# The product of the minus rows read from PSUM, a one-hot written once, powers of two for four rows at once

## The chip, the cores and the metric

The kernel runs on one core of a Trainium2 chip. Its time is the device time of one execution in microseconds (us), the median of 3 runs. Five engines work side by side and wait for each other through semaphores: PE (TensorE, matrix products; PEld is its loading of weights), DVE (VectorE), ACT (ScalarE), POOL (GpSimd) and SP (SyncE, which here only issues DMAs). PE writes its results to PSUM, eight banks of 128 x 512 float32; the other data of a core lies in SBUF.

## What is computed

```python
x  = real(fft(fft(x, axis=seq), axis=dim))       # x: 8 x 3072 x 256, float32
a, b = x @ w_a, x @ w_b                          # 256 -> 1536 each
y  = (a * b) @ w_out                             # 1536 -> 256, for 24576 rows
e  = argmax(y @ w_gate)                          # one of 8 experts for each row
out[row] = gate * sigmoid(..) * (relu(y @ w1[e]) @ w2[e])
```

## The kernel before

The first part makes, for each of 8 batches, the transform, then a and b, their product, and y with its gate; the second part (from about 2140 us) runs the experts over the rows sorted by expert. The change lies in the first part.

A real input makes the transform's rows come in pairs, position n and position S - n. From two matrix products one gets both: with U and V the two halves of a row of a, `E + O` is the row of the plus side and `E - O` the one of the minus side. So a tile is 512 positions and yields 1024 rows, 24 tiles in all, and each is worked through in 12 steps of 128 columns of a and b (f = 0 to 11), 288 steps. A step uses one of two pairs of PSUM banks, `s[0]` for a and `s[1]` for b; steps take the pairs in turn. On the engines a step (function `step`) is:

- PE: 3 products of 128x512 into the bank of a and 3 into that of b (`products(..., 0)`, L831): now the banks hold the first halves. Then `g2` (L904): 24 products of 128x256, which give y for an earlier step. Then again 3 and 3 products onto the same banks (`products(..., 1)`): now the banks hold the rows of the plus side.
- DVE, between these, for the step before (`first`) and for this one: AM[0] and AM[1] (L840), the minus rows of a and of b, each 2E less the plus row, from EE in SBUF and the bank in PSUM; hf[0] (L841), the product of the plus rows, from the bank of a and BP, a copy of the bank of b that ACT makes (L837); EE[0], EE[1] (L871), the even parts of this step's a and b, read from its banks, after which PE may write onto these banks again; hf[1] (L846, in `first_minus`), the product of the minus rows, from AM[0] and AM[1], both in SBUF.
- ACT rounds hf to float16 (L851), POOL takes the remainder hf - hl (L853, 128x1024), and `g2` of a later step uses both.

Work that belongs to other tiles or batches is dealt out beside the steps: `deal` puts an item into the first unit (a step, or one of the transform's units, called D) where its estimated costs on ACT, DVE, POOL and SP fit a budget. Such items are: the splitting of the next batch (L512 to L599), of the experts' weights (L406 to L470), and for each finished tile the rows' squares (L940), powers of two near them (`pow2`, L159 and L160), rows (L951, L957), gates (L992 to L1034) and places (L1051 to L1061). Each engine runs its instructions in the order written: within a unit the DVE's items come after hf[1].

Some of PE's items in the middle of `g2` (the logits L972, the counts L1038, the spreads L820, L388, L437) write into a bank called `aux`: the bank of a of the step before, whose last reader is hf[0].

Of the kernel before, what the change touches and what calls it, by code (L numbers as in the profile page):

```python
# [12 lines left out]
ACTF = mybir.ActivationFunctionType  # L13
ALU = mybir.AluOpType
# [27 lines left out]
def chain_kernel(ctx, tc, x, x384, w_a, w_b, w_out, w_gate, w_og, w1, w2, dft, c16, c32, ids, out):  # L42
# [11 lines left out]
    # One stretch of SBUF for the whole run: the second part keeps the experts in it,  # L54
    # the first part lays its own operands over the same places.
# [167 lines left out]
    def rows384():  # L223
        # the row that folds onto itself, of every batch: sums of its four places with their signs
# [26 lines left out]
    def from64(ts, jobs):  # L251
        # float64 to float32 by its bits; below float32's normal range it becomes 0
# [376 lines left out]
    # positions 4k, then the odd ones, then 4k + 2  # L629
# [115 lines left out]
    # the rows of position S / 2, one of each batch: all their products at once  # L745
# [63 lines left out]
    def tile_src(T):  # L809
        t, j0, nj = T  # L810
        if t == NTILE:
            return UVm, 1
        c0 = 512 * (t % 3) + 128 * j0
        return UV[:, (t // 3) % 2, :, c0:c0 + 128 * nj], 2
# [13 lines left out]
    def products(s, src, n, fs, uv):  # L828
        for ab in range(2):
            for i, (a, h) in enumerate(((0, 0), (0, 2), (1, 0))):  # L830
                pe.matmul(out=s[ab][:, 0:n], lhsT=Wt[:, ab, uv, a, fs], rhs=src[:, h + uv, :], start=(uv == 0 and i == 0), stop=(i == 2), skip_group_check=(uv == 1))  # L831

    def first(P):
        s, n, ns = P["s"], P["n"], P["ns"]
        P["hf"] = three.tile([128, 2, 512], FP32, tag="hf", name="hf")
        P["B"] = BP
        act.activation(out=P["B"][:, 0:n], in_=s[1][:, 0:n], func=ACTF.Copy)  # L837
        if ns == 2:
            for ab in range(2):
                dve.scalar_tensor_tensor(out=AM[:, ab, 0:n], in0=P["E"][:, ab, 0:n], scalar=2.0, in1=s[ab][:, 0:n], op0=ALU.mult, op1=ALU.subtract)  # L840
        dve.scalar_tensor_tensor(out=P["hf"][:, 0, 0:n], in0=s[0][:, 0:n], scalar=CA * CA, in1=P["B"][:, 0:n], op0=ALU.mult, op1=ALU.mult)  # L841

    def first_minus(P):
        n = P["n"]
        if P["ns"] == 2:
            dve.scalar_tensor_tensor(out=P["hf"][:, 1, 0:n], in0=AM[:, 0, 0:n], scalar=CA * CA, in1=AM[:, 1, 0:n], op0=ALU.mult, op1=ALU.mult)  # L846

    def second(P):
        n, ns, hf = P["n"], P["ns"], P["hf"]
        hl = hlp.tile([128, 2, 2, 512], FP16, tag="hl", name="hl")  # L850
        act.activation(out=hl[:, 0, 0:ns, 0:n], in_=hf[:, 0:ns, 0:n], func=ACTF.Copy)  # L851
        run("pool0")
        (dve if n == 128 else pool).tensor_tensor(out=hl[:, 1, 0:ns, 0:n], in0=hf[:, 0:ns, 0:n], in1=hl[:, 0, 0:ns, 0:n], op=ALU.subtract)  # L853
        hq.append((P["T"], P["f"], hl, ns))

    def step(T, f, job):
        src, ns = tile_src(T)
        n = 128 * T[2]
# [4 lines left out]
        P = {"s": s, "n": n, "ns": ns, "T": T, "f": f}  # L863
        products(s, src, n, fs, 0)
        if prev:
            first(prev[0])
        if ns == 2:
            P["E"] = EE
            c0 = 128 * T[1]
            for ab in range(2):  # L870
                dve.scalar_tensor_tensor(out=P["E"][:, ab, 0:n], in0=st_x[T[0]][:, c0:c0 + n], scalar=w0[:, ab, f:f + 1], in1=s[ab][:, 0:n], op0=ALU.mult, op1=ALU.add)  # L871
# [17 lines left out]
        products(s, src, n, fs, 1)  # L889
# [8 lines left out]
    def g2(T, f, hl, ns):  # L898
        nj = T[2]
        nt = nj * ns  # L900
# [10 lines left out]
    def post_items(T):  # L911
# [91 lines left out]
        def gate2():  # L1003
# [4 lines left out]
            oh = new("oh", 8)  # L1008
# [9 lines left out]
            if nt < 8:  # L1018
                dve.memset(oht[:, 0:8, :], 0.0)
            dve.tensor_copy(out=oht[:, 0:nt, :], in_=oh)  # L1020
# [26 lines left out]
        def place():  # L1047
# [9 lines left out]
            if first_ or t == NTILE:  # L1057
                bd = baddm if t == NTILE else badd0
                dve.tensor_tensor(out=df[:, 0:nt], in0=df[:, 0:nt], in1=bd[:, 0:nt], op=ALU.add)
            st["di"] = two.tile([128, 8], I32, tag="di", name="di")  # L1060
            dve.tensor_copy(out=st["di"][:, 0:nt], in_=df[:, 0:nt])  # L1061
# [12 lines left out]
        for a in range(0, nt, 2):  # L1074
            n_ = min(nt, a + 2) - a
            items.append((0 if a else 1, [("act", 0.43 * n_, c(square, a, a + 2)), ("dve", 0.3, c(power, a, a + 2))]))
# [192 lines left out]
    with tc.manual_schedule():  # L1269
# [4 lines left out]
        # start: the first batch and the weights  # L1274
# [160 lines left out]
        # dealing of the work beside the products  # L1435
# [63 lines left out]
        # the units  # L1499
# [366 lines left out]
```

## Time and profile before

| | |
|---|---|
| time, median of 3 (lowest to highest) | 3094.85 us (3092.26 to 3096.49) |
| span of the profiled execution | 3101.2 us |
| busy over the span: PE / DVE / ACT / POOL | 93% / 74% / 42% / 44% |
| first part: steps with L831, L871, L846 | 100 to 2025 us of the span |

The profiled execution is one more execution of the same program, with no time of its own beside the span, which runs from its first instruction to its last; so the span stands for it. It is 6.35 us over the median of the three timed runs. L12 is line 12 of the kernel; `out<-in` names the tiles that an instruction writes and reads.

### The profile page before, as it was taken

What the parts mean: (1) busy time and instruction counts of PE and PEld (TensorE: products, weight loads), DVE (VectorE), ACT (ScalarE), POOL (GpSimd) and SP (SyncE); (2) the same over time, 40 slices, a digit from 0 to 9 for tenths busy, and PEclk for the clock granted to TensorE, in tenths of its full rate; (3) what the DMA queues carried; (4) which work ended last, traced back from release to release, by engine and by line L of the source; (5) the groups of instructions that cost most, each with busy time, mean ns of one, the idle gap of its engine ahead of it and who ended that gap; (6) DMA issues with size and microseconds to landing.
All of it is one profiled execution on the core that took longest, in us unless ns stands there. A gap on an engine that the chain in (4) does not pass through costs nothing.

```text
span 3101.2 us, 62225 instructions
## 1 busy us (share of the span) xinstructions
PE 2884.3 (93%) x24101; PEld 2179.5 (70%) x24101; DVE 2293.7 (74%) x4210; ACT 1307.2 (42%) x2605; POOL 1371.9 (44%) x1083
## 2 busy tenths in 40 slices
PE   6899899989899979989989999989999999999998
PEld 3566655756566656556666666678888888888898
DVE  8779699788999778999967999935555555555556
ACT  4444455535445445445454444432333333333332
POOL 6466577465774546674524445422211111111122
PEclk8899999999999999999999999999999999999999
DMA  5321712541221362221162222445222222222211
GB/s 196 109 59 42 179 56 66 138 109 44 76 71 44 103 140 59 57 89 42 52 164 80 64 61 69 103 128 149 57 52 52 52 51 51 53 52 53 50 45 35
DMA packets 363575, 244.46 MB, mean 79 GB/s; under 512 B 303101, under 2 KB 320669, under 8 KB 362382
## 3 DMA queue, kind: packets, MB, share of 16 engines
q1 hardware_dynamic: 342158, 184.75, 24.0%
q0 software_dynamic: 18816, 51.54, 4.8%
q10 hardware_dynamic: 2304, 4.20, 0.5%
q8 instruction: 188, 3.08, 0.4%
q14 instruction: 109, 0.89, 0.1%
HBM read 106.60 MB, written 70.33 MB: 57 GB/s over the span
## 4 chain that ended last, share of the span: by engine, by line
PE 56%; DVE 23%; issue 10%; DMA 4%; ACT 3%; POOL 2%; SPq 0%; DVEq 0%; POOLq 0%; ACTq 0%
PE g L1613 16%; PE g L1637 15%; PE s L831 10%; PE y L904 10%; DVE EE L871 6%; DVE hf L846 4%; PE s L662 2%; DVE AM L840 2%; DVE ohx L1020 1%; DVE rows L957 1%; DMA big<-in_dft_dram 1%; POOL hl L853 1%; DVE hf L841 1%; ACT BP L837 1%; DMA rows<-rows,di 1%
## 5 line engine op out<-in xcount | busy, mean ns | idle before, releaser
L831 PE MATMUL s<-big 128*128 128x512 f16 x3456 | 817.3, 387 | 99.2 <-DVE EE L871 89.9
L853 POOL TENSOR_TENSOR hl<-hf,hl 128x1024 f16<-128x1024 f32 x288 | 628.5, 2182 | 576.5 <-ACT hl L851 528.8
L904 PE MATMUL y<-big,hl 128*128 128x256 f16 x6912 | 822.4, 274 | 1.2 <-POOL hl L853 1.1
L904 PEld LDWEIGHTS <-hl 128*128 128x128 f16 x6912 | 672.2, 98 | 152.6 <-issue 10.8
L831 PEld LDWEIGHTS <-big 128*128 128x128 f16 x3456 | 341.3, 99 | 476.7 <-issue 141.9
L851 ACT ACTIVATE hl<-hf 128x1024 f16<-128x1024 f32 x288 | 303.9, 1055 | 560.4 <-DVE hf L846 463.9
L1640 POOL DMA_INDIRECT out_dram<-o,di x189 | 194.3, 1028 | 777.9 <-ACT o L1639 524.6
L1613 PE MATMUL g<-yt,w1t 128*128 128x256 f16 (+1 forms) x4704 | 492.8, 265 | 3.7 <-DVE w1t L1594 3.7
L1637 PE MATMUL g<-w2t,hh 128*128 128x256 f16 x2896 | 479.5, 273 | 0.0
L1613 PEld LDWEIGHTS <-w1t 128*128 128x128 f16 x4704 | 431.5, 98 | 50.8 <-DVE w1t L1594 4.0
L840 DVE SCALAR_TENSOR_TENSOR AM<-EE,s 128x512 f32<-128x512 f32 x576 | 382.3, 681 | 111.0 <-ACT BP L837 79.3
L1616 DVE SCALAR_TENSOR_TENSOR hl<-g,hh 128x512 f16<-128x512 f32 x378 | 260.2, 691 | 239.3 <-ACT hh L1615 239.3
L1637 PE MATMUL g<-w2t,hl 128*128 128x256 f16 x1448 | 394.9, 273 | 0.0
L1615 ACT ACTIVATE hh<-g 128x512 f16<-128x512 f32 x378 | 225.0, 597 | 275.9 <-PE g L1613 275.9
L1065 POOL DMA_INDIRECT rows<-rows,di x192 | 204.1, 1063 | 266.7 <-DMA rows<-rows,di 206.7
L1637 PEld LDWEIGHTS <-hh 128*128 128x128 f16 x3024 | 294.5, 98 | 34.2
L1598 DVE COPY w2t<-big 128x4104 f16 x98 | 120.5, 1229 | 205.4 <-PE g L1637 205.4
L846 DVE SCALAR_TENSOR_TENSOR hf<-AM 128x512 f32<-128x512 f32 x288 | 266.7, 926 | 0.0
L1639 ACT ACTIVATE o<-g,sc 128x256 f32<-128x256 f32 x189 | 89.5, 473 | 410.7 <-PE g L1637 357.8
L871 DVE SCALAR_TENSOR_TENSOR EE<-big,w,s 128x512 f32<-128x512 f32 x288 | 200.8, 738 | 0.0
L871 DVE SCALAR_TENSOR_TENSOR EE<-xe,w,s 128x512 f32<-128x512 f32 x288 | 200.7, 737 | 0.0
L841 DVE SCALAR_TENSOR_TENSOR hf<-s,BP 128x512 f32<-128x512 f32 x288 | 196.2, 681 | 0.0
(330 smaller groups left out, 2859.4 us busy)
## 6 DMA issues: line engine op xcount, KB each, us to landing
big<-in_x_dram SPq DMA_DIRECT2D x48, 514.0 KB
big<-in_dft_dram SPq DMA_DIRECT2D x60, 384.0 KB
big<-in_moe_w_dram SPq DMA_DIRECT2D x16, 1024.0 KB
wsc<-big SPq DMA_DIRECT2D x32, 512.0 KB
big<-wsc SPq DMA_DIRECT2D x7, 2050.0 KB
big<-in_dft_dram SPq DMA_DIRECT2D x60, 192.0 KB
big<-wsc ACTq DMA_DIRECT2D x16, 256.2 KB
raw<-in_moe_w_out_dram SPq DMA_DIRECT2D x6, 512.0 KB
```

Of the source, the lines that this page charges most:

```text
L831: pe.matmul(out=s[ab][:, 0:n], lhsT=Wt[:, ab, uv, a, fs], rhs=src[:, h + uv, :], start=(uv == 0 and i == 0), stop=(i == 2), skip_group_che ...
L840: dve.scalar_tensor_tensor(out=AM[:, ab, 0:n], in0=P["E"][:, ab, 0:n], scalar=2.0, in1=s[ab][:, 0:n], op0=ALU.mult, op1=ALU.subtract)
L841: dve.scalar_tensor_tensor(out=P["hf"][:, 0, 0:n], in0=s[0][:, 0:n], scalar=CA * CA, in1=P["B"][:, 0:n], op0=ALU.mult, op1=ALU.mult)
L846: dve.scalar_tensor_tensor(out=P["hf"][:, 1, 0:n], in0=AM[:, 0, 0:n], scalar=CA * CA, in1=AM[:, 1, 0:n], op0=ALU.mult, op1=ALU.mult)
L851: act.activation(out=hl[:, 0, 0:ns, 0:n], in_=hf[:, 0:ns, 0:n], func=ACTF.Copy)
L853: (dve if n == 128 else pool).tensor_tensor(out=hl[:, 1, 0:ns, 0:n], in0=hf[:, 0:ns, 0:n], in1=hl[:, 0, 0:ns, 0:n], op=ALU.subtract)
L871: dve.scalar_tensor_tensor(out=P["E"][:, ab, 0:n], in0=st_x[T[0]][:, c0:c0 + n], scalar=w0[:, ab, f:f + 1], in1=s[ab][:, 0:n], op0=ALU.mul ...
L904: pe.matmul(out=Y[w // 2][:, w % 2, :], lhsT=hl[:, h, pm, 128 * j:128 * j + 128], rhs=wo[:, f, a, :], start=(f == 0 and i == 0 and w % 2 = ...
L1613: pe.matmul(out=ps[:, u, :], lhsT=w[:, a, q, 128 * f:128 * f + 128], rhs=yt[:, 2 * h + q, :], start=(m == 0), stop=(m == 5))
L1615: act.activation(out=hh[:, f0:f0 + nu, :], in_=ps, func=ACTF.Relu)
L1616: dve.scalar_tensor_tensor(out=hl[:, f0:f0 + nu, :], in0=ps, scalar=0.0, in1=hh[:, f0:f0 + nu, :], op0=ALU.max, op1=ALU.subtract)
L1637: pe.matmul(out=ps, lhsT=hx[:, f, ts], rhs=wv[:, a, f, :], start=(m == 0), stop=(m == 3 * NF2 - 1))
```

## The change

The minus row of b is no longer written to AM[1] in SBUF but in place into the bank of b in PSUM, and the product of the minus rows reads it there, with AM[0] as its other operand. AM[0] still goes to SBUF. The order becomes AM[0], hf[0], the minus row of b, EE[0], EE[1], hf[1]. The one-hot of the experts is written in float16 at once, into the tile that the counting product reads, and the later readers take it from there; the copy with a change of type (L1020) goes. The places are written as integers by the addition itself, or by a maximum of the float value with itself where nothing is added; the copy L1061 goes. The powers of two are made for four rows in a pair of instructions rather than for two. Cases for tiles other than 512 positions, which the plan doesn't make, are taken out of the step's functions.

```diff
@@ -807,11 +807,8 @@
         return cur["aux"][0]
 
     def tile_src(T):
-        t, j0, nj = T
-        if t == NTILE:
-            return UVm, 1
-        c0 = 512 * (t % 3) + 128 * j0
-        return UV[:, (t // 3) % 2, :, c0:c0 + 128 * nj], 2
+        t = T[0]
+        return UV[:, (t // 3) % 2, :, 512 * (t % 3):512 * (t % 3) + 512]
 
     def x_items(t):
         def spread():
@@ -825,50 +822,43 @@
 
         return [(0, [("pe", 1, spread), ("act", 0.6, keep_x)])]
 
-    def products(s, src, n, fs, uv):
+    def products(s, src, fs, uv):
         for ab in range(2):
             for i, (a, h) in enumerate(((0, 0), (0, 2), (1, 0))):
-                pe.matmul(out=s[ab][:, 0:n], lhsT=Wt[:, ab, uv, a, fs], rhs=src[:, h + uv, :], start=(uv == 0 and i == 0), stop=(i == 2), skip_group_check=(uv == 1))
+                pe.matmul(out=s[ab], lhsT=Wt[:, ab, uv, a, fs], rhs=src[:, h + uv, :], start=(uv == 0 and i == 0), stop=(i == 2), skip_group_check=(uv == 1))
 
     def first(P):
-        s, n, ns = P["s"], P["n"], P["ns"]
+        a, b = P["s"]
         P["hf"] = three.tile([128, 2, 512], FP32, tag="hf", name="hf")
-        P["B"] = BP
-        act.activation(out=P["B"][:, 0:n], in_=s[1][:, 0:n], func=ACTF.Copy)
-        if ns == 2:
-            for ab in range(2):
-                dve.scalar_tensor_tensor(out=AM[:, ab, 0:n], in0=P["E"][:, ab, 0:n], scalar=2.0, in1=s[ab][:, 0:n], op0=ALU.mult, op1=ALU.subtract)
-        dve.scalar_tensor_tensor(out=P["hf"][:, 0, 0:n], in0=s[0][:, 0:n], scalar=CA * CA, in1=P["B"][:, 0:n], op0=ALU.mult, op1=ALU.mult)
+        act.activation(out=BP, in_=b, func=ACTF.Copy)
+        dve.scalar_tensor_tensor(out=AM[:, 0, :], in0=EE[:, 0, :], scalar=2.0, in1=a, op0=ALU.mult, op1=ALU.subtract)
+        dve.scalar_tensor_tensor(out=P["hf"][:, 0, :], in0=a, scalar=CA * CA, in1=BP, op0=ALU.mult, op1=ALU.mult)
+        dve.scalar_tensor_tensor(out=b, in0=EE[:, 1, :], scalar=2.0, in1=b, op0=ALU.mult, op1=ALU.subtract)
 
     def first_minus(P):
-        n = P["n"]
-        if P["ns"] == 2:
-            dve.scalar_tensor_tensor(out=P["hf"][:, 1, 0:n], in0=AM[:, 0, 0:n], scalar=CA * CA, in1=AM[:, 1, 0:n], op0=ALU.mult, op1=ALU.mult)
+        dve.scalar_tensor_tensor(out=P["hf"][:, 1, :], in0=P["s"][1], scalar=CA * CA, in1=AM[:, 0, :], op0=ALU.mult, op1=ALU.mult)
 
     def second(P):
-        n, ns, hf = P["n"], P["ns"], P["hf"]
+        hf = P["hf"]
         hl = hlp.tile([128, 2, 2, 512], FP16, tag="hl", name="hl")
-        act.activation(out=hl[:, 0, 0:ns, 0:n], in_=hf[:, 0:ns, 0:n], func=ACTF.Copy)
+        act.activation(out=hl[:, 0], in_=hf, func=ACTF.Copy)
         run("pool0")
-        (dve if n == 128 else pool).tensor_tensor(out=hl[:, 1, 0:ns, 0:n], in0=hf[:, 0:ns, 0:n], in1=hl[:, 0, 0:ns, 0:n], op=ALU.subtract)
-        hq.append((P["T"], P["f"], hl, ns))
+        pool.tensor_tensor(out=hl[:, 1], in0=hf, in1=hl[:, 0], op=ALU.subtract)
+        hq.append((P["T"], P["f"], hl))
 
     def step(T, f, job):
-        src, ns = tile_src(T)
-        n = 128 * T[2]
+        src = tile_src(T)
         fs = slice(128 * f, 128 * f + 128)
         s, cur["aux"] = SB[cur["n"] % 2], SB[(cur["n"] + 1) % 2]
         cur["n"] += 1
         run("sp")
-        P = {"s": s, "n": n, "ns": ns, "T": T, "f": f}
-        products(s, src, n, fs, 0)
+        P = {"s": s, "T": T, "f": f}
+        products(s, src, fs, 0)
         if prev:
             first(prev[0])
-        if ns == 2:
-            P["E"] = EE
-            c0 = 128 * T[1]
-            for ab in range(2):
-                dve.scalar_tensor_tensor(out=P["E"][:, ab, 0:n], in0=st_x[T[0]][:, c0:c0 + n], scalar=w0[:, ab, f:f + 1], in1=s[ab][:, 0:n], op0=ALU.mult, op1=ALU.add)
+        for ab in range(2):
+            dve.scalar_tensor_tensor(out=EE[:, ab, :], in0=st_x[T[0]], scalar=w0[:, ab, f:f + 1], in1=s[ab], op0=ALU.mult, op1=ALU.add)
         if prev:
             first_minus(prev[0])
         run("early")
@@ -886,7 +876,7 @@
         run("dve")
         run("pool0")
         run("pool")
-        products(s, src, n, fs, 1)
+        products(s, src, fs, 1)
         prev.append(P)
 
     def middle():
@@ -895,9 +885,9 @@
         else:
             run("pe")
 
-    def g2(T, f, hl, ns):
+    def g2(T, f, hl):
         nj = T[2]
-        nt = nj * ns
+        nt = 2 * nj
         for w in range(nt):
             pm, j = divmod(w, nj)
             for i, (a, h) in enumerate(((0, 0), (1, 0), (0, 1))):
@@ -1005,7 +995,7 @@
             dve.scalar_tensor_tensor(out=t1, in0=st["d"], scalar=0.0, in1=rev.unsqueeze(1).to_broadcast([128, nt, 8]), op0=ALU.is_ge, op1=ALU.mult)
             mx = new("mx", 1)
             dve.tensor_reduce(out=mx, in_=t1, axis=AX.X, op=ALU.max)
-            oh = new("oh", 8)
+            oh = oht[:, 0:nt, :]
             dve.tensor_tensor(out=oh, in0=t1, in1=mx.to_broadcast([128, nt, 8]), op=ALU.is_equal)
             go_ = new("go", 8)
             dve.tensor_tensor(out=go_, in0=oh, in1=st["L"][:, :, 8:16], op=ALU.mult)
@@ -1015,9 +1005,6 @@
                 mk = mm_ if t == NTILE else m0
                 dve.tensor_tensor(out=oh, in0=oh, in1=mk[:, 0:nt].unsqueeze(2).to_broadcast([128, nt, 8]), op=ALU.mult)
             dve.tensor_scalar(out=gs[:, 0:nt], in0=gs[:, 0:nt], scalar1=-85.0, scalar2=None, op0=ALU.max)
-            if nt < 8:
-                dve.memset(oht[:, 0:8, :], 0.0)
-            dve.tensor_copy(out=oht[:, 0:nt, :], in_=oh)
             st.update(oh=oh, gs=gs)
 
         def exp2():
@@ -1054,11 +1041,9 @@
             dve.tensor_tensor(out=dst, in0=dst, in1=st["oh"], op=ALU.mult)
             df = two.tile([128, 8], FP32, tag="df", name="df")
             dve.tensor_reduce(out=df[:, 0:nt], in_=dst, axis=AX.X, op=ALU.add)
-            if first_ or t == NTILE:
-                bd = baddm if t == NTILE else badd0
-                dve.tensor_tensor(out=df[:, 0:nt], in0=df[:, 0:nt], in1=bd[:, 0:nt], op=ALU.add)
             st["di"] = two.tile([128, 8], I32, tag="di", name="di")
-            dve.tensor_copy(out=st["di"][:, 0:nt], in_=df[:, 0:nt])
+            bd, op = (baddm, ALU.add) if t == NTILE else (badd0, ALU.add) if first_ else (df, ALU.max)
+            dve.tensor_tensor(out=st["di"][:, 0:nt], in0=df[:, 0:nt], in1=bd[:, 0:nt], op=op)
 
         def scatter(w):
             def go():
@@ -1073,7 +1058,7 @@
         ]
         for a in range(0, nt, 2):
             n_ = min(nt, a + 2) - a
-            items.append((0 if a else 1, [("act", 0.43 * n_, c(square, a, a + 2)), ("dve", 0.3, c(power, a, a + 2))]))
+            items.append((0 if a else 1, [("act", 0.43 * n_, c(square, a, a + 2))] + ([("dve", 0.35, c(power, a // 4 * 4, a + 2))] if a % 4 or nt < 8 else [])))
         last = None
         for a, b in ((0, 2), (2, 5), (5, 8)):
             if a >= nt:
```

The order of instructions on ACT and on POOL is the same before and after. On DVE, one step and the gate's part of one tile, before (`s_116` and `s_114` are the banks of a of the two pairs, `s_117` and `s_115` those of b):

```order
L846 SCALAR_TENSOR_TENSOR hf<-AM 128x512
L1005 SCALAR_TENSOR_TENSOR t_7024<-d,C_72 128x64
L1007 TENSOR_REDUCE mx<-t_7024 128x8 [waits DVE_49]
L1009 TENSOR_TENSOR oh<-t_7024,mx 128x64 [waits DVE_49]
L1011 TENSOR_TENSOR go<-oh,L 128x64 [waits DVE_49]
L1013 TENSOR_REDUCE gs<-go 128x8 [waits DVE_49]
L1017 TENSOR_SCALAR gs<-gs 128x8 [waits DVE_49]
L1020 CAST ohx<-oh 128x64
L840 SCALAR_TENSOR_TENSOR AM<-EE,s_116 128x512 [waits PE_49]
L840 SCALAR_TENSOR_TENSOR AM<-EE,s_117 128x512 [waits Activation_49]
L841 SCALAR_TENSOR_TENSOR hf<-s_116,BP 128x512 [waits Pool_49]
L871 SCALAR_TENSOR_TENSOR EE<-xe,w_91,s_114 128x512 [waits DVE_49,PE_49]
```

The same place on DVE after the change:

```order
L840 SCALAR_TENSOR_TENSOR hf<-s_115,AM 128x512
L995 SCALAR_TENSOR_TENSOR t_6976<-d,C_72 128x64
L997 TENSOR_REDUCE mx<-t_6976 128x8 [waits DVE_49]
L999 TENSOR_TENSOR ohx<-t_6976,mx 128x64 [waits DVE_49]
L1001 TENSOR_TENSOR go<-ohx,L 128x64 [waits DVE_49]
L1003 TENSOR_REDUCE gs<-go 128x8 [waits DVE_49]
L1007 TENSOR_SCALAR gs<-gs 128x8 [waits DVE_49]
L835 SCALAR_TENSOR_TENSOR AM<-EE,s_116 128x512 [waits PE_49]
L836 SCALAR_TENSOR_TENSOR hf<-s_116,BP 128x512 [waits Activation_49,Pool_49]
L837 SCALAR_TENSOR_TENSOR s_117<-EE,s_117 128x512
L861 SCALAR_TENSOR_TENSOR EE<-xe,w_91,s_114 128x512 [waits DVE_49,PE_49]
```

The cast has gone; hf[0] has moved up by one place and has taken over the wait for ACT's copy; the write into `s_117` stands where hf[0] was, in front of EE.

On PE, the second products of one step (banks `s_114`, `s_115`) and the first ones of the next (`s_116`, `s_117`), before:

```order
L831 MATMUL s_115<-big 128x512 [waits DVE_49]
L831 LDWEIGHTS big
L831 MATMUL s_115<-big 128x512
L831 LDWEIGHTS big
L831 MATMUL s_115<-big 128x512
L831 LDWEIGHTS big
L831 MATMUL s_116<-big 128x512 [waits Activation_49]
L831 LDWEIGHTS big
L831 MATMUL s_116<-big 128x512
L831 LDWEIGHTS big
L831 MATMUL s_116<-big 128x512
L831 LDWEIGHTS big
L831 MATMUL s_117<-big 128x512
```

The same place on PE after the change:

```order
L828 MATMUL s_115<-big 128x512 [waits DVE_49]
L828 LDWEIGHTS big
L828 MATMUL s_115<-big 128x512
L828 LDWEIGHTS big
L828 MATMUL s_115<-big 128x512
L828 LDWEIGHTS big
L828 MATMUL s_116<-big 128x512 [waits Activation_49]
L828 LDWEIGHTS big
L828 MATMUL s_116<-big 128x512
L828 LDWEIGHTS big
L828 MATMUL s_116<-big 128x512
L828 LDWEIGHTS big
L828 MATMUL s_117<-big 128x512 [waits DVE_49]
```

The first product into the bank of b now has a wait for DVE of its own, in 256 of the steps: the bank's last reader is now hf[1] of the step before.

## Rows read from the trace of the kernel before

**Rows 1.** Stretches: us, busy PE, PEld, DVE, ACT, POOL, granted clock, DMA, GB/s.

```profile
100.00:2025.00 1925.00, 1768.35 (x13529) 1193.98 (x13530) 1656.45 (x3173) 923.25 (x1889) 1103.55 (x816) 0.98 0.30 81
...
2140.00:3101.00 961.00, 952.17 (x9066) 855.80 (x9064) 506.55 (x756) 302.23 (x545) 195.53 (x191) 1.00 0.21 51
```

**Rows 2.** The page's chain that ended last, by engine and by line.

```profile
PE 56%; DVE 23%; issue 10%; DMA 4%; ACT 3%; POOL 2%; SPq 0%; DVEq 0%; POOLq 0%; ACTq 0%
PE g L1613 16%; PE g L1637 15%; PE s L831 10%; PE y L904 10%; DVE EE L871 6%; DVE hf L846 4%; PE s L662 2%; DVE AM L840 2%; DVE ohx L1020 1%; DVE rows L957 1%; DMA big<-in_dft_dram 1%; POOL hl L853 1%; DVE hf L841 1%; ACT BP L837 1%; DMA rows<-rows,di 1%
```

**Rows 3.** Waits of PE, 100 to 2025 us: us in total, times, longest.

```profile
PE s L831 <- DVE EE L871: 89.9, 66, 3.6
...
PE s L972 <- DVE hf L841: 6.6, 7, 1.8
PE s L1038 <- DVE hf L841: 5.2, 8, 1.4
PE s L388 <- DVE hf L841: 4.9, 3, 2.1
PE s L820 <- DVE hf L841: 3.4, 3, 1.4
```

**Rows 4.** Groups of DVE's instructions: count | busy us, mean ns | idle before.

```profile
L840 DVE SCALAR_TENSOR_TENSOR AM<-EE,s 128x512 f32<-128x512 f32 x576 | 382.3, 681 | 111.0 <-ACT BP L837 79.3 <-PE s L831 27.6
L846 DVE SCALAR_TENSOR_TENSOR hf<-AM 128x512 f32<-128x512 f32 x288 | 266.7, 926 | 0.0
...
L841 DVE SCALAR_TENSOR_TENSOR hf<-s,BP 128x512 f32<-128x512 f32 x288 | 196.2, 681 | 0.0
...
L1020 DVE CAST ohx<-oh 128x64 f16<-128x64 f32 x24 | 41.5, 1731 | 0.0
...
L159 DVE TENSOR_SCALAR pq<-ssq 128x2 int32<-128x2 int32 x96 | 19.0, 198 | 17.5 <-ACT big L940 17.4
...
L160 DVE TENSOR_SCALAR r<-pq 128x2 int32<-128x2 int32 x96 | 16.5, 172 | 3.3
...
L1061 DVE CAST di<-df 128x8 int32<-128x8 f32 x24 | 14.3, 595 | 1.0 <-DVE df L1056 0.2
```

**Rows 5.** Single durations, ns: shortest/median/longest.

```profile
L846 DVE SCALAR_TENSOR_TENSOR hf<-AM x288: 671/685/3135, 100.3 to 2017.4; 128x512 f32<-128x512 f32 x144
...
L841 DVE SCALAR_TENSOR_TENSOR hf<-s,BP x288: 672/683/687, 98.4 to 2016.8; 128x512 f32<-128x512 f32 x144
...
L1020 DVE CAST ohx<-oh x24: 180/2106/2134, 239.1 to 2051.3; 128x64 f16<-128x64 f32 x24
```

**Rows 6.** Timeline, all engines, 802.6 to 806.5 us: start, duration.

```profile
802.65 2.15 POOL L853 TENSOR_TENSOR hl<-hf,hl 128x1024 f16<-128x1024 f32 x1
803.14 2.22 DVE L846 SCALAR_TENSOR_TENSOR hf<-AM 128x512 f32<-128x512 f32 x1
...
805.28 1.26 DVE L957 SCALAR_TENSOR_TENSOR rows<-tail,r,rows 128x256 f16<-128x256 f32 x3
```

**Rows 7.** Timeline, 837 to 843 us: one tile's gates on DVE.

```profile
839.60 0.17 DVE L1017 TENSOR_SCALAR gs<-gs 128x8 f32<-128x8 f32 x1
839.63 2.13 POOL L853 TENSOR_TENSOR hl<-hf,hl 128x1024 f16<-128x1024 f32 x1 [3.28 <-ACT hl L851]
839.68 2.13 DVE L1020 CAST ohx<-oh 128x64 f16<-128x64 f32 x1
```

**Rows 8.** Timeline of PE, 805 to 824 us.

```profile
809.71 2.76 PE L831 MATMUL s<-big 128*128 128x512 f16 x12 [1.71 <-DVE EE L871]
...
818.71 5.28 PE L831 MATMUL s<-big 128*128 128x512 f16 x12 [3.62 <-DVE EE L871]
```

**Rows 9.** The chain in order of time, 700 to 760 us: a stretch of PE alone.

```profile
699.96 2.51 PE y L904 x23
702.47 2.59 PE s L831 x12
```

## Prediction

> **What bounds the kernel now.** I read the stretches first. The second part, from 2140 us, has PE busy 952 of 961 us at full granted clock [rows 1], and the change touches none of it. In the first part, 100 to 2025 us, PE is busy 1768 of 1925 us and DVE 1656: neither is full, and the 157 us in which PE stands are the most that a faster DVE can give. The chain comes next: DVE has 23% of it, and the lines with most are EE, hf and AM of the step [rows 2]; where no item lies beside the steps, the chain runs through PE alone, 2.59 us for 12 products of 512 and 2.62 us for 24 of 256 [rows 9], so a step costs 5.2 us there and DVE is free to be slower. So the first part changes sides: with no items PE sets the pace, with items DVE does. The list of waits tells where that hurts: PE's second products wait for EE 89.9 us in 66 places, and the products into the lent bank of a wait for hf[0] 20.1 us in four rows (6.6 + 5.2 + 4.9 + 3.4) [rows 3]. Taken singly over PE's timeline, 110 waits of PE end on DVE, 127.9 us in all.
>
> **What DVE loses time on.** hf[1] has a median of 685 ns but a mean of 926, and one of 3135 [rows 4, 5]. hf[0], of the same size, with one operand in PSUM and one in SBUF, never takes over 687 [rows 5]. The timeline shows the difference: at 803.14 us hf[1] takes 2.22 us, begun while POOL's remainder of the step before, 802.65 to 804.80, is at work, and it ends about one undisturbed length behind it [rows 6]. The cast of the one-hot is held in the same way, and nearly always: 2106 ns at the median against 180 at its fastest [rows 5], because the remainder begins at 839.63 and the cast is ready at 839.68 [rows 7]. So DVE instructions with both operands in SBUF, and such casts, stand while POOL works; those with an operand in PSUM don't.
>
> **The change part by part.**
>
> hf[1] with an operand in PSUM takes the form of hf[0]. Held time: 266.7 us less 288 x 0.685 = 69.4 us [rows 4, 5]. This is the upper end. What is held can be handed on: behind 803.14 stands L957, which also reads SBUF twice [rows 6], and it would meet the same POOL instruction. Going through the 104 places where hf[1] takes over 0.69 us, I count all of the held time where AM comes next (it has an operand in PSUM), and at most 0.6 us where an instruction of the other kinds does, since hf[1] itself then runs inside POOL's time: 41.1 us. I take that one; it is nearer to how rows 6 read.
>
> [...]
>
> The minus row of b, written in place into PSUM. No row has a DVE instruction that writes PSUM. The nearest is the instruction it replaces, AM at 681 ns [rows 4], with the same operands and another output. Below, 671 ns is the shortest of this size [rows 5]: 288 x 0.010 = 2.9 us of DVE gained. Above, a second pass through the bank would be twice 681: 196 us lost. I take 681, zero change, and keep the upper end as a rival.
>
> The cast's removal gives up to 41.5 us of DVE, 24 instructions [rows 4]. Nothing but the step's AM follows it in the place shown, which POOL does not hold. The one-hot's own instruction now writes 16 bits; I cost that at nothing (24 x 0.05 us would be 1.2).
>
> Powers of two: 96 pairs become 48. 96 x (198 + 172) ns = 35.5 us [rows 4], half of it 17.8 us. Two columns more per instruction I cost at nothing; even 20 ns on each of the 96 left would be 1.9 us.
>
> Places: L1061's cast, 595 ns at the mean [rows 4], is replaced by an instruction with two SBUF operands at the same place. It can be held as the cast was. I count zero; all of its time, 14.3 us, is the other end.
>
> The order. hf[0] ends one instruction earlier, 0.68 us, so the lent bank of a is free earlier; against this the bank of b is now read until hf[1]. Its next writer is PE's fourth product of the next step. That comes behind the three of the second b products and three into the bank of a, 6 x 0.216 = 1.3 us (2.59 / 12 each [rows 9]) after EE[1] at the earliest, and hf[1] needs 0.68 us from there: covered by 0.6 us as long as POOL doesn't hold it, which it no longer can. Behind that product on PE stands g2, so a lost cover would cost its whole excess. ACT's and DVE's waits for BP are the same: AM[1] waited for it, now hf[0] does, at the same time, with the same four instructions behind it to the end of EE[1].
>
> **The sum.** DVE gets 41.1 + 41.5 + 17.8 = 100 us (129 with hf[1] uncapped). PE feels only what falls on its waits. I laid each of the 110 waits beside the savings that lie on DVE since the wait before, with 0.6 us more where the wait is for hf[0], and took the smaller of the two. An example: the wait of 1.71 us at 809.71 [rows 8] has behind it the hf[1] of 803.14; uncapped its 1.54 us would come off, capped 0.6 [rows 6]. The wait of 3.62 us at 818.71 [rows 8] stands behind L957 and gets 0.05. All together: 51.3 us. Of it the order alone (hf[0] earlier) gives 15.4, with the powers 25.1, with hf[1] 41.1, with the cast 51.3. Half of what DVE saves is lost because PE is the bound there.
>
> The profiled execution has 3101.2 us, so 3050 in its own terms; it lies 6.35 us over the median, and on the median it is 3094.85 - 51.3 = 3044 us.
>
> **The rivals.**
>
> Further: the savings that exceed a wait are not lost, since DVE comes into the next step earlier. With up to 1 us carried from one wait to the next the same count gives 73.9 us: 3021. For it: waits with no saving of their own often follow close on one with too much. [...] Against it: in the PE-bound steps DVE cannot start AM before PE is done, so a lead dies out.
>
> Handed on: POOL's remainder meets another instruction in nearly all places. In the gates, L1017 begins 0.03 us before POOL does [rows 7]; were it that little later, it would be held in the cast's place, and the pow2 and L957 behind hf[1] likewise. Then only the order and the powers stay, 25.1 us: 3070. For it: the thin 0.03 us. Against it: nothing ahead of L1017 gets longer.
>
> Slower: the write into PSUM takes two passes, 1.36 us. EE is on the chain 271 times, that is in some 135 of 288 steps; there 0.68 us each are 92 us lost, less 51 gained: 41 slower, 3136. It decides from 0.38 us per write on (51 / 135). Against it: every row that reads PSUM costs what one of SBUF costs [rows 5]. [...] No run here shows DVE writing PSUM.
>
> No change: the waits of PE are taken over by ACT's rounding and POOL's remainder, so that y's products come late instead of EE. Then under 6 of the 128 us come off: 3091. Against it: in the first part POOL and ACT are busy 1104 and 923 of 1925 us [rows 1].
>
> **How the numbers follow.** The forecast 0.52, further 0.20, handed on 0.16, slower 0.07, no change 0.05. Further, the forecast and handed on span 3021 to 3070; with 6 to 8 us on either side for the sizes left open (the places, the write's lower end, half a dozen us of granted clock) the range is 3014 to 3078 us, which leaves out the two last cases and some of the tails. What this kernel's measurement can't tell from no change is 0.2%, 6.2 us. Faster: 0.52 + 0.20 + 0.16, less a little for a handed-on case that ends near nothing, 0.87; same 0.05; slower 0.08.
>
> **What would show it.** hf[1] should have a median near 683 and no duration over 0.75 us; the write into `s` 681; no group of ohx casts, and L1007 (the former L1017) still at 0.17 to 0.33 us at the mean; 48 pairs of powers. PE's wait for EE should fall from 89.9 to about 60 us, that for hf[0] to a quarter. POOL's and ACT's busy times should stay. Wrong it would be if the write takes over 1 us, if PE's fourth product waits for hf[1], or if L957, L1007 and the powers grow by what hf[1] and the cast lost.

## The result, and the profile after

The changed kernel takes 3058.01 us (median of 4 runs, 3054.62 to 3059.24) against 3095.67 us (4 runs, 3092.26 to 3098.67) for the kernel before on the same chip: ratio 0.9873 [0.9858, 0.9889], so 37.7 us faster. The forecast was 3044 us, a gain of 51. The sign and the range held; the gain was a quarter smaller, and it came from other terms than forecast. Line numbers shift by a few from kernel to kernel; a group is known by its tiles (`hf<-...`).

First the stretches of the kernel after: first part, then second part (us, busy PE, PEld, DVE, ACT, POOL, granted clock, DMA share, GB/s).

```profile
100.00:1985.00 1885.00, 1766.49 (x13546) 1200.52 (x13547) 1575.25 (x3053) 935.31 (x1906) 1068.20 (x816) 0.98 0.31 84
2100.00:3055.00 955.00, 946.33 (x9021) 852.15 (x9018) 505.03 (x754) 300.44 (x541) 195.40 (x189) 1.00 0.22 51
```

PE has the same work in the first part as in [rows 1] and stands 118.5 us instead of 156.7: 38.2 us less. The second part is full as before. The chain that ended last has changed sides: PE from 56% to 75%, DVE from 23% to 11% [rows 2].

```profile
PE 75%; DVE 11%; issue 7%; DMA 3%; ACT 2%; POOL 0%; SPq 0%; DVEq 0%; POOLq 0%; ACTq 0%
PE s L828 19%; PE y L894 18%; PE g L1598 16%; PE g L1622 15%; PE s L662 3%; DVE EE L861 2%; DVE s L837 2%; DVE rows L947 1%; DVE hf L840 1%; DMA big<-in_dft_dram 1%; DVE AM L835 1%; DMA rows<-rows,di 1%; PE s L962 1%; ACT BP L834 1%; PE s L289 1%
```

PE's waits of the first part on the step's instructions (us in total, times, longest):

```profile
PE s L828 <- DVE EE L861: 66.8, 34, 6.1
...
PE s L1025 <- DVE hf L836: 3.7, 3, 1.6
PE s L437 <- DVE hf L836: 3.6, 2, 2.6
...
PE s L817 <- DVE hf L836: 2.3, 2, 1.1
...
PE s L962 <- DVE hf L836: 0.4, 1, 0.4
```

The wait for EE fell by 23.1 us. That for hf[0] fell from 20.1 to 6.4 us in the lines of [rows 3] (L1025, L817 and L962 here; the fourth, L388, waits no longer); L437's, 2.4 us before, is 3.6. The first two together are 36.8 of the 38.2 us. But look at the first row's other two numbers: half as many waits, 34 for 66, and the longest is 6.1 us where it was 3.6. What is left is rarer and bigger. DVE's groups (count | busy us, mean ns | idle before) show why:

```profile
L836 DVE SCALAR_TENSOR_TENSOR hf<-s,BP 128x512 f32<-128x512 f32 x288 | 198.3, 688 | 112.9 <-ACT BP L834 102.7 <-ACT eg L1012 6.8 <-POOL big L534 0.8
L837 DVE SCALAR_TENSOR_TENSOR s<-EE,s 128x512 f32<-128x512 f32 x288 | 197.0, 684 | 0.0
L840 DVE SCALAR_TENSOR_TENSOR hf<-s,AM 128x512 f32<-128x512 f32 x288 | 196.6, 683 | 0.2
L947 DVE SCALAR_TENSOR_TENSOR rows<-tail,r,rows 128x256 f16<-128x256 f32 x192 | 147.5, 818 | 0.0
L465 DVE SCALAR_TENSOR_TENSOR big<-big,r2e 128x512 f16<-128x512 f32 x32 | 23.5, 747 | 0.2 <-ACT big L459 0.2
L159 DVE TENSOR_SCALAR pq<-ssq 128x4 int32<-128x4 int32 x48 | 17.6, 367 | 19.9 <-ACT big L930 19.8
...
L160 DVE TENSOR_SCALAR r<-pq 128x4 int32<-128x4 int32 x48 | 8.6, 179 | 1.7
...
L1007 DVE TENSOR_SCALAR gs<-gs 128x8 f32<-128x8 f32 x24 | 6.0, 252 | 0.5
```

Single durations (shortest/median/longest, ns) of the write into `s`, of hf[1] and of the rows' low parts:

```profile
L837 DVE SCALAR_TENSOR_TENSOR s<-EE,s x288: 674/685/689, 101.2 to 1973.1; 128x512 f32<-128x512 f32 x144
...
L840 DVE SCALAR_TENSOR_TENSOR hf<-s,AM x288: 672/684/692, 103.1 to 1973.8; 128x512 f32<-128x512 f32 x144
...
L947 DVE SCALAR_TENSOR_TENSOR rows<-tail,r,rows x192: 462/479/5442, 204.2 to 1993.4; 128x256 f16<-128x256 f32 x192
```

hf[1] is never held any more: mean 683 ns for 926 [rows 4], longest 692 for 3135 [rows 5]. The write in place into PSUM costs what its predecessor did, 684 ns for 681. But L947, the line that stood behind the held hf[1] in [rows 6], grew to 147.5 us at 818 ns. The same group and its single durations before:

```profile
L957 DVE SCALAR_TENSOR_TENSOR rows<-tail,r,rows 128x256 f16<-128x256 f32 x192 | 99.4, 567 | 0.0
...
L957 DVE SCALAR_TENSOR_TENSOR rows<-tail,r,rows x192: 466/478/2350, 204.2 to 2038.8; 128x256 f16<-128x256 f32 x192
```

Of the 70 us that hf[1] gave up, 48 are here. The first instruction of a pair of powers has 367 ns for four rows where it took 198 for two. DVE's busy time fell by 84 us in all (2293.7 to 2209.5). POOL's, which was to stay, fell by 36 (1371.9 to 1335.7); this was not followed up.

One place of the kernel after, timeline of all engines (start, duration; in brackets idle before and what ended it). A tile's eight rows come in groups of two, three and three; `x3` is the middle group:

```profile
783.75 2.15 POOL L847 TENSOR_TENSOR hl<-hf,hl 128x1024 f16<-128x1024 f32 x1
783.87 0.68 DVE L840 SCALAR_TENSOR_TENSOR hf<-s,AM 128x512 f32<-128x512 f32 x1
784.47 7.48 DVE L947 SCALAR_TENSOR_TENSOR rows<-tail,r,rows 128x256 f16<-128x256 f32 x3
...
786.06 1.00 POOL L1050 DMA_INDIRECT rows<-rows,di  x1 [0.17 <-issue]
...
787.08 2.14 POOL L847 TENSOR_TENSOR hl<-hf,hl 128x1024 f16<-128x1024 f32 x1
...
789.17 1.28 POOL L519 TENSOR_TENSOR big<-big 128x512 f32<-128x512 f32 x1
790.39 1.26 POOL L520 TENSOR_TENSOR big<-big 128x508 f32<-128x508 f32 x1
791.60 0.40 POOL L521 COPY big<-big 128x4 f32<-128x4 f32 x1
791.87 0.74 DVE L465 SCALAR_TENSOR_TENSOR big<-big,r2e 128x512 f16<-128x512 f32 x1
...
795.11 4.72 PE L828 MATMUL s<-big 128*128 128x512 f16 x12 [6.09 <-DVE EE L861]
```

hf[1] at 783.87 goes through POOL's remainder unhindered. The three instructions of L947 behind it took 1.72, 0.47 and 5.44 us: the first stands until that remainder ends; the third begins at 786.50 while POOL is at a scatter, and then stands through the next remainder and through L519 and L520, which POOL runs back to back, to 791.9. Behind it come L465, the step's three instructions L835 to L837 and EE[0], and PE stands 6.09 us, the longest wait of the table. Such a wait costs more than itself. The window of the products behind it (same columns as the stretches):

```profile
795.10:799.90 4.80, 4.79 (x15) 1.86 (x15) 4.80 (x10) 2.26 (x3) 2.35 (x1) 0.58 0.48 142
```

The granted clock is 0.58 there, where it is 0.98 over the first part, and 12 products take 4.72 us instead of 2.76 [rows 8]. Behind six of the seven waits for EE of over 3 us in this kernel the 12 products take 4.1 to 5.3 us, at a granted clock of 0.50 to 0.65, behind the seventh 2.76 at 1.00. In 11 of the 24 tiles the third row of this group takes 3.0 us or more, and each of the 11 begins some 0.44 us into a scatter with the remainder right behind it (two meet the splittings too, 5.43 and 5.44 us). Taken singly, PE's next wait for EE behind these 11 rows is 1.8 to 6.1 us, 37.3 of the 66.8 us in all. Of the group's 48 us more, 32 lie on this row, which meets POOL's next instructions, and 15 on the first row of the group, which stands until the remainder beside hf[1] ends.

hf[1] lost its held time when one operand moved to PSUM (longest 692 ns for 3135); L947, which reads two from SBUF, did not (longest 5442 ns for 2350).

### The profile page after: what moved, and what is told of

Its sections match the earlier page's. It is cut to its first block, busy times and chain, and to the rows that moved or that the text cites. A ratio compares the mean times of both kernels' runs of the same rounds, so it can differ in the third digit from the quotient of the medians.

```text
span 3055.4 us, 62396 instructions
## 1 busy us (share of the span) xinstructions
PE 2881.0 (94%) x24101; PEld 2184.9 (72%) x24101; DVE 2209.5 (72%) x4079; ACT 1315.1 (43%) x2605; POOL 1335.7 (44%) x1083
## 4 chain that ended last, share of the span: by engine, by line
PE 75%; DVE 11%; issue 7%; DMA 3%; ACT 2%; POOL 0%; SPq 0%; DVEq 0%; POOLq 0%; ACTq 0%
PE s L828 19%; PE y L894 18%; PE g L1598 16%; PE g L1622 15%; PE s L662 3%; DVE EE L861 2%; DVE s L837 2%; DVE rows L947 1%; DVE hf L840 1%; DMA big<-in_dft_dram 1%; DVE AM L835 1%; DMA rows<-rows,di 1%; PE s L962 1%; ACT BP L834 1%; PE s L289 1%
## 5 line engine op out<-in xcount | busy, mean ns | idle before, releaser
L828 PE MATMUL s<-big 128*128 128x512 f16 x3456 | 824.9, 389 | 74.1 <-DVE EE L861 66.8
L847 POOL TENSOR_TENSOR hl<-hf,hl 128x1024 f16<-128x1024 f32 x288 | 626.4, 2175 | 566.2 <-ACT hl L845 422.9
L1050 POOL DMA_INDIRECT rows<-rows,di x192 | 191.7, 998 | 264.4 <-DMA rows<-rows,di 199.2
L835 DVE SCALAR_TENSOR_TENSOR AM<-EE,s 128x512 f32<-128x512 f32 x288 | 195.9, 680 | 30.7 <-PE s L828 28.3
L834 ACT ACTIVATE BP<-s 128x512 f32<-128x512 f32 x288 | 170.2, 591 | 67.6 <-PE s L828 64.3
```

The lines of the kernel that those rows point to most:

```text
L828: pe.matmul(out=s[ab], lhsT=Wt[:, ab, uv, a, fs], rhs=src[:, h + uv, :], start=(uv == 0 and i == 0), stop=(i == 2), skip_group_check=(uv = ...
L834: act.activation(out=BP, in_=b, func=ACTF.Copy)
L835: dve.scalar_tensor_tensor(out=AM[:, 0, :], in0=EE[:, 0, :], scalar=2.0, in1=a, op0=ALU.mult, op1=ALU.subtract)
L847: pool.tensor_tensor(out=hl[:, 1], in0=hf, in1=hl[:, 0], op=ALU.subtract)
```

## The experiments

Each ratio is against the kernel before, run beside it (medians of 3097.4 to 3098.6 us).

**Each part alone, in the kernel before.** Order and PSUM operand together (the instructions written as formulas, B for the copy of b):

```diff
-        for ab in range(2): AM[:, ab] = 2 * E[:, ab] - s[ab]     # both, ahead of hf[0]
+        AM[:, 0] = 2 * E[:, 0] - s[0]
         hf[:, 0] = s[0] * B
+        s[1] = 2 * E[:, 1] - s[1]                                # in place
-        hf[:, 1] = AM[:, 0] * AM[:, 1]
+        hf[:, 1] = s[1] * AM[:, 0]
```

> The kernel before with the step's part of the change alone: minus row of b in place in PSUM and read there by hf[1], hf[0] moved up. My theory (held time of hf[1] goes, part of it is handed on to the rows): hf[1] at 683 ns in all 288, its 70 us of held time gone from it, the rows' group up from 99 us by 20 to 50 us, time 3095 less 20 to 35 us. The order theory (only hf[0] earlier matters): less 15 us, and the same as the kernel with the order alone. The cast theory (only the cast mattered): no change.

Measured 3093.02 us, 0.9986 [0.9974, 0.9997]. DVE's groups and PE's longest group of waits in this run:

```profile
L845 DVE SCALAR_TENSOR_TENSOR hf<-s,AM 128x512 f32<-128x512 f32 x288 | 196.0, 680 | 0.2
L956 DVE SCALAR_TENSOR_TENSOR rows<-tail,r,rows 128x256 f16<-128x256 f32 x192 | 137.8, 766 | 0.0
...
L159 DVE TENSOR_SCALAR pq<-ssq 128x2 int32<-128x2 int32 x96 | 27.8, 289 | 17.7 <-ACT big L939 17.5
```
```profile
PE s L831 <- DVE EE L870: 93.1, 52, 6.4
```

hf[1] is freed and PE's wait for EE is no shorter than the 89.9 of [rows 3]; the 20 to 35 us that were expected did not come. L956 and the powers' first instructions take 38.4 and 8.8 us more.

The order without the PSUM operand (the same edit, but the minus row of b stays `AM[:, 1]`, in SBUF):

> The kernel before with the new order alone: AM[0], hf[0], AM[1], both minus rows in SBUF as before. My theory: PE's waits for hf[0] fall from 25 us to under 12 us, hf[1] is held as before (mean near 926 ns), time less 5 to 15 us. The order theory: all that the step's part gives, 15 us or more. Rival (the order is worth nothing, since EE ends at the same time): within 3 us of before.

Measured 3090.65 us, 0.9974 [0.9963, 0.9985]. hf[1] is held as before:

```profile
L845 DVE SCALAR_TENSOR_TENSOR hf<-AM 128x512 f32<-128x512 f32 x288 | 260.6, 905 | 0.2
```

So the order is worth some 8 us, about half of its 15.4, and the PSUM operand on top of it nothing: 3093.0 against 3090.7. DVE does have less to do with the operand in PSUM, 2271.8 us against 2291.9 over the whole execution; those 20 us do not reach PE.

The casts alone (in part; the rest of this edit stands in the diff of the change):

```diff
-            oh = new("oh", 8)
+            oh = oht[:, 0:nt, :]
             ...
-            dve.tensor_copy(out=oht[:, 0:nt, :], in_=oh)
             ...
-            dve.tensor_copy(out=st["di"][:, 0:nt], in_=df[:, 0:nt])
+            dve.tensor_tensor(out=st["di"][:, 0:nt], in0=df[:, 0:nt], in1=bd[:, 0:nt], op=op)
```

> The kernel before with the one-hot and the places written without casts alone. My theory: 41 us leave DVE, PE feels 16 us (prediction's count for the cast alone), range 8 to 25; the last gate instruction L1017 stays under 0.35 us at the mean. Rival (handed on): L1017 or the next is held by POOL in its place, its group goes from 8 to over 40 us, and the time stays within 4 us.

Measured 3065.39 us, 0.9897 [0.9883, 0.9911]: 32 us, by far the largest part, and over the 8 to 25 that were expected. DVE's group that could have inherited the held time, and PE's wait:

```profile
L1017 DVE TENSOR_SCALAR gs<-gs 128x8 f32<-128x8 f32 x24 | 9.1, 381 | 0.5
```
```profile
PE s L831 <- DVE EE L871: 61.0, 46, 3.6
```

The gates' last instruction, 0.03 us from being held in [rows 7], has 9.1 us in all (before 7.9); the 41.5 us of the cast [rows 4] are really gone (DVE as a whole is busy 48 us less, 2245.2 for 2293.7), and PE's wait for EE falls by 28.9 us.

The powers alone (one pair for every four rows, as in the change):

> The kernel before with the powers for four rows at once alone. My theory: 18 us less on DVE, some 5 to 11 us less time. Rival (the wider pairs only wait longer for ACT's squares, or meet POOL): no change within 4 us, with the 48 pairs costing as much as the 96 did.

Measured 3094.06 us, 0.9991 [0.9979, 1.0003]: 3 us, not told from none.

The parts multiply: 0.9986 (order and operand) x 0.9897 x 0.9991 = 0.9874, the whole's 0.9873.

**One part taken back, in the kernel after.** The minus row of b back in SBUF (`out=AM[:, 1, :]`, and hf[1] from `AM[:, 0, :]` and `AM[:, 1, :]`):

> The changed kernel with the minus row of b back in SBUF (order, casts and powers stay changed). By now the theory is: the cast carries the gain, and what hf[1] no longer loses is taken over by the rows behind it, in fewer and longer holds (13 of some 3 to 5 us behind a scatter and POOL's remainder). By it the time is that of the changed kernel, 3058 within 8 us, with hf[1] held 65 us again and the rows back near 20 us of held time. Rival (the PSUM operand adds its own part, 41 us of DVE, once the cast is gone): 3075 to 3085.

Measured 3057.53 us, 0.9863 [0.9845, 0.9881]: the same as the kernel after.

```profile
L840 DVE SCALAR_TENSOR_TENSOR hf<-AM 128x512 f32<-128x512 f32 x288 | 269.7, 936 | 0.2
...
L947 DVE SCALAR_TENSOR_TENSOR rows<-tail,r,rows 128x256 f16<-128x256 f32 x192 | 103.7, 589 | 0.0
```
```profile
PE s L828 <- DVE EE L861: 64.0, 49, 3.6
```

This pair of kernels is the plainest view of what was handed on: hf[1] 73.1 us more, L947 43.8 less, PE's wait for EE 64.0 in 49 places against 66.8 in 34. DVE's busy time is 25 us longer (2234.7 against 2209.5), and the time is the same.

The powers back to pairs of two rows:

> The changed kernel with the powers for two rows at once, as before. Theory: the powers are worth some 3 us, so 3061 within 5 us, rows held as in the changed kernel. Rival (the powers' place sets when the rows come, and so whether they meet POOL): rows' held time under 40 us and a time more than 8 us from 3058.

Measured 3054.81 us, 0.9851 [0.9832, 0.9871], not the 3061 expected: the interval overlaps that of the kernel after, so the powers bring nothing that can be measured there either.

**Moving the row that is held.** In the kernel after, the fifth row's low part is done with the last group of rows instead of the middle one:

```diff
+            lo, hi = (a - (a > 2), b - (b == 5)) if nt == 8 else (a, b)
             ...
-            ("dve", 0.38 * m, c(row_lo, a, b))
+            ("dve", 0.38 * m, c(row_lo, lo, hi))
             ...
-            last = c(turn, a, b)
+            last = c(turn, lo, hi)
```

> The changed kernel with the low part of a tile's fifth row (the third of the middle group, the one that is held 3 to 5 us) made with the last group, one or more units later; ACT's and POOL's work as before. Theory (these holds take back what hf[1] gave): the rows' held time falls from 65 to under 30 us, PE's waits for EE from 67 to some 40 us, none above 4; time 3058 less 20 to 35 us. Rival (handed on once more, to the next row or to another instruction of the same kind): held time of all DVE within 10 us of 132, time within 6 us of 3058. Rival (PE is the bound, held time costs nothing now): held time falls, time stays.

Measured 3059.79 us, 0.9873 [0.9855, 0.9892]: no gain.

```profile
L947 DVE SCALAR_TENSOR_TENSOR rows<-tail,r,rows 128x256 f16<-128x256 f32 x192 | 119.8, 672 | 0.0
L465 DVE SCALAR_TENSOR_TENSOR big<-big,r2e 128x512 f16<-128x512 f32 x32 | 51.7, 1629 | 0.3 <-ACT big L459 0.2
```

L947 gave up 27.7 us and L465, the next instruction with two SBUF operands, took 28.2. Handed on once more. The same move in the kernel before:

> The kernel before with the same move of the fifth row. Theory: there the rows are held 17 us only, behind other POOL work, so nothing is won: within 5 us of 3098. Rival (the move is good by itself, whatever hf[1] does): 15 us or more faster.

Measured 3105.79 us, 1.0025 [1.0013, 1.0037]: slightly slower; there the fifth row was not the one held (at most 0.86 us in any tile).

**Taking POOL's side away.** In the kernel with the minus row in SBUF, and in the kernel after, POOL's remainder is replaced by a zero-fill; these two kernels leave out what the remainders add to y:

```diff
-        pool.tensor_tensor(out=hl[:, 1], in0=hf, in1=hl[:, 0], op=ALU.subtract)
+        pool.memset(hl[:, 1], 0.0)
```

> The kernel with order, casts and powers changed but both minus rows in SBUF, and POOL's remainder (hf less its rounded value) left out: POOL writes zeros there and reads nothing. Theory (holds behind the remainder cost time wherever they fall, so the PSUM operand only moved them): hf[1]'s held time falls from 73 us to under 25 us, and the time by 15 us or more from 3057. Rival (held time of 0.2 to 2 us is covered by PE, so it never cost anything, and only the long ones behind the gates did): held time falls as much, the time stays within 6 us of 3057.

> The changed kernel with POOL's remainder left out in the same way. Theory: the rows' held time falls from 66 to under 30 us; time 15 us or more under 3058, and within 6 us of the kernel with both minus rows in SBUF and the remainder left out, since then nothing holds hf[1] in either. Rival (rows are held by the scatters, not by the remainder): rows' held time stays over 50 us, time stays.

Measured 2987.45 us, 0.9620 [0.9596, 0.9644], and 2970.54 us, 0.9593 [0.9576, 0.9609]. First the kernel with the operand in SBUF, then the one with it in PSUM:

```profile
L840 DVE SCALAR_TENSOR_TENSOR hf<-AM 128x512 f32<-128x512 f32 x288 | 208.2, 723 | 0.2
```
```profile
PE s L828 <- DVE EE L861: 28.1, 21, 2.9
```
```profile
L947 DVE SCALAR_TENSOR_TENSOR rows<-tail,r,rows 128x256 f16<-128x256 f32 x192 | 85.1, 498 | 0.3 <-issue 0.3
```
```profile
PE s L828 <- DVE EE L861: 13.8, 14, 2.9
```

With the remainder gone hf[1] has 723 ns even with two SBUF operands, and L947 498. Taken singly, 21 of these hf[1] begin inside a zero-fill, and none takes over 686 ns; those still held, up to 2.03 us, begin inside a splitting. So it is the subtraction that holds them. The kernels are 70 us (3057.5 - 2987.5) and 87 (3058.0 - 2970.5) faster. How much of that is held time is not shown: POOL's instruction is also shorter, 959 ns instead of 2175, and no longer waits for ACT's rounding. Between these two kernels the PSUM operand is worth 17 us by the medians and 8 by the ratios, where at most 6 was expected; their intervals just overlap. Whether it pays where nothing behind it can be held is not settled by this.

**Another order, to take hf[1] out of POOL's way.** In the kernel with the minus row in SBUF, hf[1] and what follows from it (ACT's rounding, POOL's remainder) are moved behind the step's items on DVE:

```diff
-        if prev: first_minus(prev[0])
         run("early")
         ...
-        if prev: second(prev.pop())
         run("dve0")
         run("dve")
+        if prev: first_minus(prev[0]); second(prev.pop())
```

> Order, casts and powers changed, minus rows in SBUF; in a step the DVE's items now stand ahead of hf[1] rather than behind it, when the remainder of the step before should be over, and hf[1], ACT's rounding and POOL's remainder follow the items. Theory (what counts is whether the items meet POOL): held time of rows, gates and splittings falls under 40 us in all, hf[1] is held more often; time 5 to 25 us under 3057. Rival (POOL is late anyway in the steps with scatters and the remainder now comes 1 to 2 us later): held time within 20 us of 162, time 3057 or above.

Measured 3209.65 us, 1.0363 [1.0345, 1.0380]. Waits of ACT, DVE and PE:

```profile
ACT hl L845 <- DVE hf L840: 818.3, 275, 6.1
```
```profile
DVE hf L836 <- ACT BP L834: 236.0, 250, 2.3
```
```profile
PE s L828 <- DVE EE L861: 147.7, 127, 4.0
```

hf[1] has 746 ns and L946, the rows' low parts, 540, so most of the held time went and DVE is busy 38 us less (2196.5 for 2234.7); yet the kernel lost 152 us against the one it was made from (3057.5); the rival had the sign (3057 or above), but with the held time as it was. ACT's rounding now waits for a late hf[1] (435.8 us in that kernel); the copy of b for the next step stands behind it on ACT; hf[0] waits for that copy, 236.0 us for 90.3; and EE, behind hf[0], comes late for PE (147.7 us for 64.0).

**The cast kept, but two instructions earlier**, ahead of the reduction and the gates' last instruction, in the kernel before (arguments shortened):

```diff
+            dve.tensor_copy(out=oht[:, 0:nt, :], in_=oh)
             dve.tensor_reduce(out=gs[:, 0:nt], in_=go_, axis=AX.X, op=ALU.add)
             dve.tensor_scalar(out=gs[:, 0:nt], ..., scalar1=-85.0, ..., op0=ALU.max)
-            dve.tensor_copy(out=oht[:, 0:nt, :], in_=oh)
```

> The kernel before with the cast of the one-hot two places earlier, ahead of the reduction and of the last gate instruction L1017 (here L1020). No instruction goes. Theory (the cast cost what it did because it was the one instruction of its kind that stood just behind the start of POOL's remainder; the last gate instruction is of the kind that POOL holds): the cast's held time falls under 10 us, that of the last gate instruction rises from 4 to 30 us or more, time within 6 us of 3097. Rival (it isn't held): both under 10 us, time some 30 us less, as without the cast.

Measured 3087.33 us, 0.9963 [0.9951, 0.9975]: 11 us of the cast's 32, more than the 6 expected at most.

```profile
L1020 DVE TENSOR_SCALAR gs<-gs 128x8 f32<-128x8 f32 x24 | 19.7, 821 | 0.8
...
L1018 DVE CAST ohx<-oh 128x64 f16<-128x64 f32 x24 | 8.4, 352 | 0.3
```

The cast is held, for some 2 us, in 2 of 24 places instead of 19, 33.1 us less; the gates' last instruction takes its place in 9, with 1.85 to 2.12 us each for 0.17 alone (19.7 us in all for 7.9). So a `tensor_scalar` in that spot is held as a cast is. DVE as a whole is busy 18 us less than before (2275.5), where the run without casts had 48 less: other groups took over some of the rest, and the gains of 11 and 32 us stand in nearly the same proportion.

## Why the prediction was right in sign and too large

**hf[1], the term that failed.** "I count all of the held time where AM comes next (...), and at most 0.6 us where an instruction of the other kinds does": 41.1 us of DVE, 16 us of the sum. hf[1] behaved as said, and the term is worth nothing here: in the kernel before 3093.0 against 3090.7, in the kernel after 3058.0 against 3057.5. The cap asked what the instruction next in line would meet of the *same* POOL instruction. But DVE, once earlier, meets POOL's *next* ones: in the timeline the third L947 begins inside a scatter and is held through the remainder and two splittings that follow. DVE as a whole got 20 to 25 us back and not 41.1, and PE nothing of it: fewer holds, longer ones, and over half of PE's wait for EE stands behind the 11 long ones. That is the rival "handed on" for this one part; a sign that the prediction named for being wrong, L957 growing by what hf[1] lost, came for 48 of 70 us.

**The cast, undersized.** The sum gave it its last 10 us, counted alone it was 16; measured 32 of its 41.5 us. "Took the smaller of the two" assumed that a saving larger than the next wait is lost. A cast's hold saves some 2 us at once, and it may be that what the next wait did not need came off a later one: the same count done again over the trace of before, for the cast alone, gives 16 us with nothing carried and 32 with up to 1 us carried, as in the rival "further". That agreement is one number; for the whole change the rival's 73.9 is twice what was measured. The thin 0.03 us ahead of L1017 did hold: 252 ns in the kernel after.

**The order.** Counted 15.4, measured 8: in the run with the order alone the waits for hf[0] in the lines of [rows 3] were halved (20.1 to 10.7 us), not quartered, and the wait for EE did not fall (99.4 us for 89.9).

**The powers.** About 10 us counted, 3 measured, not told from none. In the run with the powers alone DVE got 13 us back (2280.7 for 2293.7) and PE's wait for EE stayed at 89.6; in the whole change the pairs are held more often too, 367 ns for 198.

**Places.** Counted zero. Their instruction has a mean of 525 ns in 16 of 24 tiles, held as expected.

**The write into PSUM.** 684 ns, as taken; the slower rival was wrong from its first number. PE's fourth product does not wait for hf[1]: no row of PE's waits in the first part names L840.

Forecast were 15.4 (order) + 9.7 (powers) + 16.0 (hf[1]) + 10.2 (cast) = 51.3 us; measured alone some 8 + 3 + 0 + 32 (39 in all by the run that has order and operand together), and 37.7 in the whole. That errors of both signs left a gain near the forecast is luck: the place of the gain was misjudged more than its size.

Left open: why the row that begins at 786.50 is not let in before the remainder. Alone it would have ended at 786.98, 0.10 us ahead of the remainder, and the row before it passed through the same scatter in 0.47 us. Whether a row begun at another moment of the scatter would pass was not tried. Open too is why 13 us less of DVE (the powers) brought 3 us and 48 less (the casts) 32; for hf[1] the long holds are an answer. No kernel tested that computes everything beats the one after beyond its interval.

## What to carry to other kernels

Held time between two engines belonged here to the place in the queue more than to the instruction that showed it: before counting its removal, ask whether the next instruction is of the same kind, and what the other engine runs after the one in the trace. Removing the instruction altogether where nothing of that kind follows it (the cast) paid 32 us; making it immune where others follow (hf[1]) paid nothing. Judge by the waits of the engine that sets the pace, their number and their longest, and not by the mean of the one group that was changed. The held time over all groups is not enough either: DVE had 25 us less to do with the operand in PSUM, and the time was the same.

## What was not expected of the hardware

A DVE instruction of 0.48 us was held for 5.44 us (L947), another of 0.75 us for 5.7 (L465 with the row moved), through several POOL instructions that follow each other without a gap; the longest hold of hf[1] before had been 3.1 us in all [rows 5]. A `scalar_tensor_tensor` of 128x512 in place in PSUM takes as long as one that writes SBUF: 684 and 681 ns. And POOL's zero-fill of 128x1024 left a two-operand instruction alone (at most 686 ns in the 21 places where hf[1] began inside it), where its subtraction held hf[1] to a median of 1.79 us in 52 such places of the kernel with the operand in SBUF.
